# Two column tiles of 256 columns instead of four of 128 in the last two products of a decode step, with two stores for one and four loads of x for five

## The chip, the cores and the metric

The kernel runs on one core of a Trainium2 chip. The metric is the device time of one execution in microseconds (us), given as the median of several runs. A profile is one execution recorded by the hardware; its span is the part between the first and the last recorded work, and the execution's own time is a little longer. The engines are named as in the profile: PE is TensorE (matmul), PEld its weight loads, DVE is VectorE, ACT is ScalarE, POOL is GpSimd and SP is SyncE, which here only issues DMAs. "SPq" and "ACTq" are the instruction queues of SP and ACT as they issue DMAs.

## The reference

One decode step for a batch of 8 rows of 512 numbers, all in bfloat16:

```
xn = layernorm(x)                                   # x: 8 x 512
q  = xn @ wq                                        # 512 x 4096: 32 heads of 128
s  = softmax(q k^T / sqrt(128)) v, last 1024 keys   # 8 key/value heads, each for 4 query heads
s  = s.reshape(8, 4096) @ wo                        # wo: 4096 x 512
f  = (gelu(xn @ w_gate) * (xn @ w_up)) @ w_down     # 512 x 1792, 512 x 1792, 1792 x 512
out = x + s * silu(f)                               # 8 x 512
```

The keys and values that are read are 16 MB each, wq and wo 4 MB each, and the three weights of the second branch 1.75 MB each.

## The kernel before

The order of work on each engine is the order of the program (`tc.manual_schedule()`); nothing reorders it. Tiles in on-chip memory come from pools, and a load into a reused buffer waits until the old content has been read.

**Loads.** ACT issues x first, in five loads of two, two, two, one and one rows (L78, L79). SP issues everything else, in order, on one DMA queue: the first quarter of wo (`wo_first`, L106), wq whole (L109), then the keys and values of the eight batch rows in pieces of 1 MB (`load_cache`, L81 to L90), then w_gate, w_up and w_down (L438, L441), then the rest of wo: two quarters whole and the last in pieces of 5, 2 and 1 of its eight slices (L447 to L451). The large tiles go round in eight buffers (`slot`). The framework has eight semaphores for DMAs and gives them out in turn to the DMAs of the whole program, so that a DMA is not issued before the one eight places ahead of it has landed.

**Layernorm and queries.** DVE takes mean and variance of x (L145, L147), ACT the root (L149), DVE normalizes (L152). PE transposes the result (L167), and spreads x itself over partitions with a matmul (L172) whose result ACT keeps as `x_res` (L179): row b of column block t sits on partition 32t + 4b. The queries are 32 matmuls of 512 columns (L261).

**Attention.** For each batch row: DVE turns the keys over (L249), PE makes the scores (L311), DVE and ACT the softmax (L321 to L333), PE multiplies by the values (L355), and a regrouping on PE and DVE (L376 to L407) leaves the heads' outputs as the stationary operand `oT`.

**The end.** w_gate and w_up are multiplied in four column tiles of 448 columns (L465). A column tile is a stationary operand of 32 columns that uses a quarter of PE's columns, and four of them, with the results on partitions 0, 32, 64 and 96, can run at once. The gelu is a chain of ACT and DVE operations (L475 to L488) that gives `hT`. The product with w_down (L491 to L500) has 14 steps of four column tiles with 128 columns each into `f_ps`. ACT and DVE make silu of it (`g_sb`, L502 to L506). The product with wo (L509 to L519) has 32 steps of the same form into `s_ps`, eight for each quarter of wo. Then DVE multiplies `s_ps` by `g_sb` (L521) and adds `x_res` (L523), and SP stores the result in one DMA that collects 8 rows of 128 columns from each of four partition groups (L525).

Of the kernel before, what the change touches and what calls it, by code (L numbers as in the profile page):

```python
# [10 lines left out]
BF16 = mybir.dt.bfloat16  # L11
FP32 = mybir.dt.float32
# [4 lines left out]
RB = 4  # L17
# [4 lines left out]
def kernel(  # L22
# [13 lines left out]
    nc = tc.nc  # L36

    B, Sq, D = A_x.shape
# [7 lines left out]
    P = nc.NUM_PARTITIONS  # L46
# [4 lines left out]
    ROW = C * Dh  # L51
    FT = F // 4
    NJ = F // P
    DT = D // 4

    ctx.enter_context(tc.manual_schedule())
    consts = ctx.enter_context(tc.tile_pool(name="consts", bufs=1))
    keep = ctx.enter_context(tc.tile_pool(name="keep", bufs=1))
# [16 lines left out]


    x_sb = keep.tile([B, D], BF16, name="x_sb")
    for r, z in ((0, 2), (2, 4), (4, 6), (6, 7), (7, 8)):  # L78
        nc.scalar.dma_start(out=x_sb[r:z], in_=A_x.flatten_outer_dims()[r:z])  # L79

    def load_cache(cache, b, name):  # L81
# [15 lines left out]
    def load_v(b):  # L97
# [21 lines left out]
        out=ident,  # L119
        in_=ident,  # L120
# [13 lines left out]
        out=xpad,  # L134
        in_=xpad,
# [17 lines left out]
        out=xhat,  # L153
# [3 lines left out]
        op0=ALU.subtract,  # L157
        op1=ALU.mult,
    )
    x_res = keep.tile([P, DT], FP32, name="x_res")  # L160
    warm = keep.tile([B, 1], FP32, name="warm")
    nc.scalar.activation(out=warm, in_=rstd, func=ACT.Exp)  # L162
    with tc.tile_pool(name="ps_x", bufs=1, space=PSUM) as ps_x:
        xnT_ps = ps_x.tile([P, NK, B], BF16, name="xnT_ps")
        xv = xhat.rearrange("b (p k) -> b k p", k=NK)
        for k in range(NK):
            nc.tensor.transpose(xnT_ps[:, k, :], xv[:, k, :], ident[0:B, 0:B])  # L167
        for j in range(4):
            nc.vector.tensor_copy(out=xnR[:, :, j, 0 : RB * B : RB], in_=xnT_ps)
        xr_ps = ps_x.tile([P, DT], FP32, name="xr_ps")  # L170
        for t in range(4):
            nc.tensor.matmul(  # L172
                xr_ps[32 * t : 32 * t + 32, :],
                xpad,
                x_sb[:, t * DT : (t + 1) * DT],
                start=True,
                stop=True,
            )
        nc.scalar.copy(out=x_res, in_=xr_ps)  # L179
# [10 lines left out]
        out=hv,  # L190
        in_=hv,
# [7 lines left out]
        out=neg_st,  # L199
        in_=neg_st,  # L200
# [8 lines left out]
        out=neg_mv,  # L209
        in_=neg_mv,  # L210
# [11 lines left out]
    for g in range(NG):  # L222
        nc.vector.tensor_reduce(
            out=sel[:, g, g * qd : (g + 1) * qd],
            in_=ident.rearrange("p (t g h) -> p g h t", t=4, g=NG)[:, g],
# [5 lines left out]
        out=own, in_=ident.rearrange("p (i e) -> p e i", e=8), axis=AX.X, op=ALU.add  # L231
    )
    pick = consts.tile([P, 4 * NU], BF16, name="pick")
    with nc.allow_low_precision(reason="sums of zeros and a single one"):
        nc.vector.tensor_reduce(
            out=pick, in_=ident.rearrange("p (a e) -> p a e", e=8), axis=AX.X, op=ALU.add
# [20 lines left out]
    with tc.tile_pool(name="ps_q", bufs=1, space=PSUM) as ps_q:  # L257
# [10 lines left out]
        for half in range(2):  # L268
            for i in range(4 * half, 4 * half + 4):
                e = nc.vector.tensor_copy if i % 4 == 3 else nc.scalar.copy  # L270
# [7 lines left out]
    for j in range(4):  # L278
        sl = slice(32 * j, 32 * j + 32)
        for m in range(2):  # L280
            for g in range(NG):
                e = nc.scalar.copy if (4 * j + 2 * m + g) % 3 == 2 else nc.vector.tensor_copy
# [160 lines left out]
    for u in range(1, NU):  # L443
        if u % 2 == 1:
            pair = slot("wo_sb").rearrange("p (v j d) -> p v j d", v=2, d=D)
        t = pair[:, (u - 1) % 2]
# [11 lines left out]
    ps_f = ctx.enter_context(tc.tile_pool(name="ps_f", bufs=1, space=PSUM))  # L458
    ffn = ctx.enter_context(tc.tile_pool(name="ffn", bufs=1))
    zu = []  # L460
    for n, ws in (("z_ps", wgu[0]), ("u_ps", wgu[1])):
# [15 lines left out]
        out=z2, in0=z2, scalar1=0.044715, scalar2=1.0, op0=ALU.mult, op1=ALU.add  # L477
# [10 lines left out]
    nc.vector.transpose(  # L488
        out=hT.rearrange("p j b -> p (j b)"), in_=h_bf.rearrange("p (y j) -> p j y", j=NJ)
    )  # L490
    f_ps = ps_f.tile([P, DT], FP32, name="f_ps")  # L491
    for j in range(NJ):
        for t in range(4):
            nc.tensor.matmul(
                f_ps[32 * t : 32 * t + 32, :],
                hT[:, j, :],
                wd[:, j, t * DT : (t + 1) * DT],
                start=(j == 0),
                stop=(j == NJ - 1),
            )  # L500
    g_sb = ffn.tile([P, DT], FP32, name="g_sb")
    nc.scalar.activation(out=g_sb, in_=f_ps, func=ACT.Tanh, scale=0.5)  # L502
    nc.vector.tensor_scalar(
        out=g_sb, in0=g_sb, scalar1=0.5, scalar2=0.5, op0=ALU.mult, op1=ALU.add
# [1 line left out]
    nc.vector.tensor_tensor(out=g_sb, in0=g_sb, in1=f_ps, op=ALU.mult)  # L506


    s_ps = ps_f.tile([P, DT], FP32, name="s_ps")  # L509
    for u in range(NU):  # L510
        for j in range(8):
            for t in range(4):
                nc.tensor.matmul(  # L513
                    s_ps[32 * t : 32 * t + 32, :],
                    oT[:, j, u, :],
                    wo[u][:, j, t * DT : (t + 1) * DT],
                    start=(u == 0 and j == 0),
                    stop=(u == NU - 1 and j == 7),
                )  # L519
    y = ffn.tile([P, DT], FP32, name="y")  # L520
    nc.vector.tensor_tensor(out=y, in0=s_ps, in1=g_sb, op=ALU.mult)  # L521
    out_sb = ffn.tile([P, DT], BF16, name="out_sb")
    nc.vector.tensor_tensor(out=out_sb, in0=y, in1=x_res, op=ALU.add)  # L523
    out_f = out.flatten_outer_dims()
    nc.sync.dma_start(  # L525
        out=out_f.rearrange("b (t d) -> t b d", t=4), in_=out_sb[0 : P : RB, :]
    )


# [28 lines left out]
```

## Time and profile before

| | |
|---|---|
| median of 3 runs | 120.95 us (120.84 to 121.92) |
| the profiled execution's own time | 120.88 us |
| its span | 119.0 us |
| mean granted PE clock | 0.887 of full speed |
| busy share of the span: PE, DVE, ACT, POOL | 61%, 64%, 26%, 3% |
| moved by DMA | 47.60 MB, mean 400 GB/s |

The span is what the views of the profile divide up. The 1.9 us between the span and the own time of the execution lie outside of the record. A row of the timeline has the start in us, the time in us, the engine, the line, the operation, what it writes and reads, how many instructions are merged in the row and, in brackets, how long the engine had been idle and what ended that. A row of the windows view has, for a stretch of time, the busy us of each engine with its instructions in flight, then the granted PE clock as a share of full speed, the mean busy share of the 16 DMA engines, and the GB/s that they moved. Where the page speaks of packets, these are the single pieces that a DMA engine moves; a packet of 4 bytes is the semaphore update at the end of a DMA.

### The profile page before, as it was taken

What the parts mean: (1) busy time and instruction counts of PE and PEld (TensorE: products, weight loads), DVE (VectorE), ACT (ScalarE), POOL (GpSimd) and SP (SyncE); (2) the same over time, 40 slices, a digit from 0 to 9 for tenths busy, and PEclk for the clock granted to TensorE, in tenths of its full rate; (3) what the DMA queues carried; (4) which work ended last, traced back from release to release, by engine and by line L of the source; (5) the groups of instructions that cost most, each with busy time, mean ns of one, the idle gap of its engine ahead of it and who ended that gap; (6) DMA issues with size and microseconds to landing.
All of it is one profiled execution on the core that took longest, in us unless ns stands there. A gap on an engine that the chain in (4) does not pass through costs nothing.

```text
span 119.0 us, 2306 instructions
## 1 busy us (share of the span) xinstructions
PE 72.0 (61%) x992; PEld 37.5 (32%) x992; DVE 75.8 (64%) x101; ACT 31.4 (26%) x75; POOL 3.2 (3%) x10
## 2 busy tenths in 40 slices
PE   0000079941599596979964875698399264844650
PEld 0000033410133253545532434244135253414530
DVE  1000487999999999999957995971994224165100
ACT  1300230096202417170531421151070800120000
POOL 2000052000000000000000000000000000000000
PEclk9999999999679999999999999689859955578595
DMA  2998999999999999999999999999999999999930
GB/s 72 458 507 375 391 421 424 435 427 427 427 430 419 424 435 419 427 430 416 432 424 424 421 430 427 419 435 421 427 424 427 440 434 430 419 431 416 415 138 3
DMA packets 6109, 47.60 MB, mean 400 GB/s; under 512 B 716, under 2 KB 852, under 8 KB 1108
## 3 DMA queue, kind: packets, MB, share of 16 engines
q1 hardware_dynamic: 6084, 47.46, 94.6%
q8 instruction: 7, 0.11, 0.3%
q14 instruction: 2, 0.02, 0.0%
q10 hardware_dynamic: 16, 0.01, 0.0%
HBM read 47.46 MB, written 0.01 MB: 399 GB/s over the span
## 4 chain that ended last, share of the span: by engine, by line
DMA 61%; DVE 15%; PE 15%; ACT 3%; issue 2%; ACTq 1%; DVEq 0%
DMA wo_sb<-in_A_wo_dram 19%; DMA k_sb<-in_A_k_cache_dram 17%; DMA v_sb<-in_A_v_cache_dram 17%; DMA x_sb<-in_A_x_dram 9%; PE q_ps L261 7%; PE S_ps L311 6%; DVE kT L249 6%; DVE qbd L284 2%; DVE mx L321 2%; DVE q_both L274 1%; ACT P_sb L333 1%; ACTq L79 1%; ACT L162 1%; DVE q_both L271 1%; PE O_ps L355 1%
## 5 line engine op out<-in xcount | busy, mean ns | idle before, releaser
L311 PE MATMUL S_ps<-kT,qbd 128*128 128x512 bf16 x128 | 34.8, 420 | 15.4 <-DVE kT L249 12.0
L249 DVE STREAM_TRANSPOSE kT<-k_sb 128x2048 int32<-128x2048 int32 x16 | 36.6, 2289 | 5.0 <-DMA k_sb<-in_A_k_cache_dram 4.9
L311 PEld LDWEIGHTS <-qbd 128*128 128x128 bf16 x128 | 13.0, 103 | 33.3 <-issue 18.0
L331 ACT ACTIVATE nb<-m 32x1 f32<-32x1 f32 x32 | 6.4, 201 | 22.9 <-DVE m L328 22.6
L333 ACT ACTIVATE P_sb<-S_ps,nb 128x1024 bf16<-128x1024 f32 x8 | 11.1, 1391 | 0.3
L355 PE MATMUL O_ps<-v_sb,pT 128*32 128x128 bf16 x512 | 9.5, 231 | 2.6 <-DVE pT L344 2.6
L321 DVE TENSOR_REDUCE mx<-S_ps 128x1 f32<-128x1024 f32 x8 | 9.6, 1195 | 1.7 <-PE S_ps L311 1.6
L355 PEld LDWEIGHTS <-pT 128*32 128x32 bf16 x512 | 8.0, 103 | 5.6 <-issue 3.0
L261 PE MATMUL q_ps<-wq_sb,xnR 128*128 128x512 bf16 x32 | 9.2, 460 | 0.5 <-ACT x_res L179 0.5
L167 PE MATMUL xnT_ps<-ident,xhat 8*128 8x8 bf16 x4 | 0.3, 174 | 15.0 <-DVE xhat L152 15.0
L368 ACT COPY O_sb<-O_ps 128x256 f32<-128x256 f32 x8 | 3.0, 372 | 23.7 <-PE O_ps L355 23.7
L145 DVE BATCH_NORM_STATS2 stats<-x_sb 8x6 f32<-8x512 bf16 x1 | 0.7, 683 | 11.8 <-DMA x_sb<-in_A_x_dram 11.8
L344 DVE STREAM_TRANSPOSE pT<-P_sb 128x512 int32<-128x512 int32 x8 | 5.7, 711 | 3.4 <-ACT P_sb L333 3.3
L376 PE MATMUL o_ps<-O_sb,sel 128*32 128x128 f32 x32 | 5.4, 296 | 1.0 <-ACT O_sb L368 1.0
L300 PE MATMUL S_ps<-neg_mv,neg_st 128*128 128x512 bf16 x16 | 4.8, 381 | 1.9 <-DVE q_both L271 1.9
L261 PEld LDWEIGHTS <-xnR 128*128 128x128 bf16 x32 | 3.6, 114 | 5.8 <-issue 3.0
L271 ACT CAST q_both<-q_ps 128x512 bf16<-128x512 f32 x6 | 3.0, 613 | 7.9 <-PE q_ps L261 7.9
L167 PEld LDWEIGHTS <-xhat 8*128 8x128 bf16 x4 | 0.2, 114 | 15.0 <-DVE xhat L152 15.0
L376 PEld LDWEIGHTS o_ps<-O_sb,sel 128*32 128x32 f32 x32 | 3.0, 115 | 4.7 <-issue 3.2
L513 PE MATMUL s_ps<-wo_sb,oT 128*32 128x128 bf16 x96 | 2.7, 252 | 2.2 <-DMA wo_sb<-in_A_wo_dram 2.2
L252 DVE MEMSET qbd<- 128x4096 uint32 x1 | 3.5, 3472 | 0.8 <-issue 0.8
L513 PEld LDWEIGHTS <-oT 128*32 128x32 bf16 x128 | 3.0, 123 | 2.8 <-issue 2.6
(65 smaller groups left out, 51.1 us busy)
## 6 DMA issues: line engine op xcount, KB each, us to landing
k_sb<-in_A_k_cache_dram SPq DMA_DIRECT2D x16, 1024.0 KB, 19.7
v_sb<-in_A_v_cache_dram SPq DMA_DIRECT2D x16, 1024.0 KB, 19.8
wq_sb<-in_A_wq_dram SPq DMA_DIRECT2D x1, 4096.0 KB, 14.2
wo_sb<-in_A_wo_dram SPq DMA_DIRECT2D x2, 1024.0 KB
wgu_sb<-in_B_w_gate_dram SPq DMA_DIRECT2D x1, 1792.0 KB
wgu_sb<-in_B_w_up_dram SPq DMA_DIRECT2D x1, 1792.0 KB
wd_sb<-in_B_w_down_dram SPq DMA_DIRECT2D x1, 1792.0 KB, 25.1
wo_first<-in_A_wo_dram SPq DMA_DIRECT2D x1, 1024.0 KB, 4.8
```

Of the source, the lines that this page charges most:

```text
L249: nc.vector.transpose(out=t.bitcast(I32), in_=k_sb[b][:, g].bitcast(I32))
L261: nc.tensor.matmul(q_ps[i], xnR[:, k, :, :].rearrange("p j b -> p (j b)"), wq_sb[k][:, i * 512 : (i + 1) * 512], start=(k == 0), stop=(k = ...
L271: e(out=q_bf[:, i * 512 : (i + 1) * 512], in_=q_ps[i])
L300: nc.tensor.matmul(S[b][:, half, :], neg_st.rearrange("p j h -> p (j h)"), neg_mv.rearrange("p a n -> p (a n)"), start=True, stop=False,)
L311: nc.tensor.matmul(S[b][:, half, :], qbd[:, m, b, w, g, :], kv[:, half * 16 : (half + 1) * 16, m, :, w], start=False, stop=(g == NG - 1 an ...
L321: nc.vector.tensor_reduce(out=mx, in_=S[b].rearrange("p a c -> p (a c)"), axis=AX.X, op=ALU.max)
L331: nc.scalar.mul(nb[32 * j : 32 * j + 32, :], m1, -inv)
L333: nc.scalar.activation(out=P_sb[b].rearrange("p c i w -> p c w i"), in_=S[b].rearrange("p a (c w i) -> p (a c) w i", w=2, i=32), func=ACT.Exp,
L344: nc.vector.transpose(out=pT[b].rearrange("p c h w -> p (c h w)").bitcast(I32), in_=P_sb[b].rearrange("p c i w -> p (c i w)").bitcast(I32),)
L355: nc.tensor.matmul(O_ps[b][32 * t : 32 * t + 32, g, :], pT[b][:, c // 2, :, c % 2], vv[:, c, :], start=(c < 4), stop=(c >= C - 4),)
L376: nc.tensor.matmul(o[:, 0:Dh], sel[:, g, :], O_sb[b][:, g, :], start=(g == 0), stop=(g == NG - 1))
L513: nc.tensor.matmul(s_ps[32 * t : 32 * t + 32, :], oT[:, j, u, :], wo[u][:, j, t * DT : (t + 1) * DT], start=(u == 0 and j == 0), stop=(u = ...
```

## The change

The number of column tiles in the products with w_down and wo goes from four to two, and their width from 128 columns to 256. All tiles that follow from it (`x_res`, `xr_ps`, `f_ps`, `g_sb`, `s_ps`, `y`, `out_sb`) go from 128 x 128 to 64 x 256. The store becomes two stores of 8 rows and 256 columns, one issued by SP and one by ACT. The last two loads of x, of one row each, become one of two rows. The products with w_gate and w_up keep their four column tiles.

```diff
-    DT = D // 4
+    NT = 2
+    DT = D // NT
...
-    for r, z in ((0, 2), (2, 4), (4, 6), (6, 7), (7, 8)):
+    for r, z in ((0, 2), (2, 4), (4, 6), (6, 8)):
         nc.scalar.dma_start(out=x_sb[r:z], in_=A_x.flatten_outer_dims()[r:z])
...
-    x_res = keep.tile([P, DT], FP32, name="x_res")
+    x_res = keep.tile([32 * NT, DT], FP32, name="x_res")
...
-        xr_ps = ps_x.tile([P, DT], FP32, name="xr_ps")
-        for t in range(4):
+        xr_ps = ps_x.tile([32 * NT, DT], FP32, name="xr_ps")
+        for t in range(NT):
...
-    f_ps = ps_f.tile([P, DT], FP32, name="f_ps")
+    f_ps = ps_f.tile([32 * NT, DT], FP32, name="f_ps")
     for j in range(NJ):
-        for t in range(4):
+        for t in range(NT):
...
-    g_sb = ffn.tile([P, DT], FP32, name="g_sb")
+    g_sb = ffn.tile([32 * NT, DT], FP32, name="g_sb")
...
-    s_ps = ps_f.tile([P, DT], FP32, name="s_ps")
+    s_ps = ps_f.tile([32 * NT, DT], FP32, name="s_ps")
     for u in range(NU):
         for j in range(8):
-            for t in range(4):
+            for t in range(NT):
...
-    y = ffn.tile([P, DT], FP32, name="y")
+    y = ffn.tile([32 * NT, DT], FP32, name="y")
     nc.vector.tensor_tensor(out=y, in0=s_ps, in1=g_sb, op=ALU.mult)
-    out_sb = ffn.tile([P, DT], BF16, name="out_sb")
+    out_sb = ffn.tile([32 * NT, DT], BF16, name="out_sb")
     nc.vector.tensor_tensor(out=out_sb, in0=y, in1=x_res, op=ALU.add)
     out_f = out.flatten_outer_dims()
-    nc.sync.dma_start(
-        out=out_f.rearrange("b (t d) -> t b d", t=4), in_=out_sb[0 : P : RB, :]
-    )
+    for t, e in ((0, nc.sync), (1, nc.scalar)):
+        e.dma_start(
+            out=out_f[:, t * DT : (t + 1) * DT], in_=out_sb[32 * t : 32 * t + 32 : RB, :]
+        )
```

## The prediction

> **What bounds the kernel now.** I read the page's chain of work first, then the windows view for the DMA share and the granted clock, then the timeline of the last 11 us, and at last the waits and the rows of the tiles that the change touches.
>
> ```profile
> DMA 61%; DVE 15%; PE 15%; ACT 3%; issue 2%; ACTq 1%; DVEq 0%
> ...
> 20.00:30.00 10.00, 5.86 (x26) 2.23 (x23) 9.77 (x15) 5.24 (x10) 0.00 (x0) 1.00 1.01 427
> 60.00:70.00 10.00, 6.78 (x94) 3.57 (x94) 7.70 (x9) 3.09 (x9) 0.00 (x0) 1.00 1.01 424
> 100.00:110.00 10.00, 5.16 (x100) 2.87 (x104) 5.23 (x8) 1.12 (x2) 0.00 (x0) 0.67 1.00 424
> 114.00:115.20 1.20, 0.55 (x26) 0.40 (x26) 0.00 (x0) 0.00 (x0) 0.00 (x0) 1.00 0.36 128
> ```
>
> The last two columns of the windows are the DMA share and GB/s. From 20 to 110 us every stretch has a share of about 1.0 and 424 to 433 GB/s, whatever the other engines do, and the stream ends at 115.1. So the time is the stream plus what is left to do after its last piece. A load of keys lands 17.2 to 20.3 us after its issue (rows of k_sb), so some 17 us of loads are always queued.
>
> ```profile
> 105.00:106.00 1.00, 0.47 (x8) 0.00 (x0) 0.36 (x2) 0.58 (x1) 0.00 (x0) 0.60 0.98 420
> 109.00:110.00 1.00, 1.00 (x60) 1.00 (x52) 0.00 (x0) 0.00 (x0) 0.00 (x0) 0.60 1.03 434
> 112.00:113.00 1.00, 0.08 (x8) 0.08 (x11) 0.00 (x0) 0.00 (x0) 0.00 (x0) 0.69 1.04 415
> ```
>
> The column before the DMA share is the clock. It is 0.50 or 1.00 and changes inside these three stretches: up at 105.8, down at 109.2, up at 112.6, steps of 3.4 us.
>
> ```profile
> 108.80 1.35 PE L494 MATMUL f_ps<-wd_sb,hT 128*32 128x128 bf16 x56 [3.33 <-DVE hT L488]
> 109.92 1.08 PE L513 MATMUL s_ps<-wo_first,oT 128*32 128x128 bf16 x32
> 110.78 1.08 PE L513 MATMUL s_ps<-wo_sb,oT 128*32 128x128 bf16 x32
> 112.92 0.63 PE L513 MATMUL s_ps<-wo_sb,oT 128*32 128x128 bf16 x32 [1.06 <-DMA wo_sb<-in_A_wo_dram]
> 114.47 0.46 PE L513 MATMUL s_ps<-wo_sb,oT 128*32 128x128 bf16 x20 [0.92 <-DMA wo_sb<-in_A_wo_dram]
> 115.11 0.57 PE L513 MATMUL s_ps<-wo_sb,oT 128*32 128x128 bf16 x12 [0.18 <-DMA wo_sb<-in_A_wo_dram]
> 115.73 0.29 DVE L521 TENSOR_TENSOR y<-s_ps,g_sb 128x128 f32<-128x128 f32 x1 [4.61 <-PE s_ps L513]
> 116.06 0.29 DVE L523 TENSOR_TENSOR out_sb<-y,x_res 128x128 bf16<-128x128 f32 x1
> 116.38 0.70 SPq L525 DMA_DIRECT2D out_dram<-out_sb  x1
> ```
>
> PE waits three times for wo, 2.16 us in all: that is its whole slack. The last piece of wo releases the last four matmuls at 115.44, DVE adds two operations, and the store is issued from 116.38 to 117.08. The trace's packet records have its 32 packets of 256 bytes from 117.68 to 117.84 and the last update at 117.86. SP sees it at 118.21, and 0.8 us of closing work ends the span.
>
> **The change, part by part.** The sum is made against the profiled execution, 120.88 us, which is 0.07 under the median of 120.95.
>
> The PE products. Eight steps of four tiles take from 109.92 to 110.78, 0.107 us a step at clock 0.50; at 112.92, (0.63 - 0.22 of the last matmul) over nearly eight steps, 0.055 us at 1.00. A 512-column matmul (L311) takes 1.91 us for eight at full clock, (1.91 - 0.38)/7 = 0.219, four times as much: the step goes by columns. Two tiles of 256 columns then cost 0.213 us a step at half clock and 0.107 at full. There are 14 + 32 = 46 steps. With the clock as in this execution: from 108.80 to 109.20 at full clock 3.8 steps, to 112.62 at half clock 16, so w_down ends at 111.4 and the first half of wo is partly done; the other 26.2 steps at full clock take 2.8 us, to 115.4. The last piece comes at 115.44. So the slack is used up nearly to the last step, and the end moves only by the longer last step: +0.05. Cover gone, it would cost the 46 steps' doubling, 2.5 us at full clock and 4.9 at half. g_sb would be ready near 113.0 (f_ps at 111.8, then ACT and two DVE operations of 0.3 to 0.43), 2.7 us before L521 needs it; today it is ready at 111.1.
>
> The two last DVE operations have 256 columns instead of 128. The same operation takes 0.29 us on 128 columns and 0.62 on 448 (L479, L483), 1.03 ns a column, so each becomes 0.42. Both are on the path: +0.27. L502, L503 and L506 grow likewise behind the wait for wo, at nothing; cover gone, 0.3.
>
> The store. The issue has 0.70 us for 4 x 8 pieces. Nearest rows for a plain one: ACT's loads of two rows, 0.24 to 0.27 us, the first of them 0.54; SP's loads of 128 rows, 0.33. I take 0.33 on SP, nearest in engine and place, and 0.24 to 0.54 on ACT, beside it. From end of issue to first packet 0.60 here, and 0.39 for the first load of x; I keep 0.60. The packets: 32 on four engines (four updates) in 0.17 us become eight of 512 bytes in each store, one to an engine if it follows the old pattern; a packet of 1024 bytes takes 0.046 us, so 0.05 with its update, -0.12. In sum -0.37 - 0.12, and 0.04 back for a second store among the closing waits (SP's waits stand 0.06 apart): -0.45. Bounds: -0.79 (issue 0.24, latency 0.39, packets 0.05) and +0.1 (ACT at 0.54 or more, a wait more, the rest unchanged). ACT has nothing queued behind its store, and its last work before, g_sb, is long done.
>
> The Trainium skill speaks against this gain: "DMA: Bandwidth & Descriptors", section "Anatomy of one DMA", puts the fixed cost of a small DMA at about 2 us, nearly all of it the receipt of the last byte. Here the store takes 1.83 us from issue to SP's release, near that, but 0.70 of it is the issue and only 0.35 comes after the last packet.
>
> x in four loads.
>
> ```profile
> L79 ACTq DMA_DIRECT2D x_sb<-in_A_x_dram x5: 243/273/542, 0.8 to 2.3; - x5
> ...
> SPq L84 <- DMA x_sb<-in_A_x_dram: 5.1, 3, 1.9
> ...
> 16.03 4.43 PE L261 MATMUL q_ps<-wq_sb,xnR 128*128 128x512 bf16 x10 [0.52 <-ACT x_res L179]
> ...
> DMA to landing us min/median/max: 14.2/14.2/14.2
> ```
>
> The issues end at 2.6, and x is complete only at 12.7: in the packet records each load of x has its rows, and 1.2 us later its update, between the large packets of wo and wq; the fourth load has its row at 8.95 and its update at 10.20, the fifth at 11.41 and 12.66. Without the fifth, x is there 2.5 us sooner. But the queries also need wq, which lands 14.2 us after its issue at 1.26, at 15.46, and today they start at 16.03. So at most 0.57 us is won there, and the stream, with 17 us of loads queued, hides it: 0. Cover gone, it is worth -0.2 (the matmuls run at half clock until 20.5 anyway) to -0.57. SP's early loads waited 5.1 us for landings of x, through the shared semaphores; one load less lets some go 1 to 2 us sooner, into a full queue: 0. The steady spacing of eight DMAs in flight is the same. L172 and L179 have half the instructions or twice the columns, long before they are needed: 0.
>
> Sum: 120.88 + 0.05 + 0.27 - 0.45 = 120.75, on the median's scale 120.8. The likeliest case reaches from 120.4 to 121.2 with the store's bounds.
>
> **Rivals.**
> *The clock's steps fall elsewhere.* The steps of 3.4 us need not stand the same to the program each time. A step with PE 78% busy (109.2 to 112.6) was followed by full clock, one with 72% (95.6 to 99.0) was not. If the step that begins after PE's start at 108.8 begins at 109.5 to 111.4, the clock is half from 108.8 to 112.9 to 114.8, and the 46 steps end 0.2 to 1.1 us behind the last piece of wo: 121.0 to 121.9. Chance 0.25. For the forecast speaks that this profile's own phase gives no delay.
>
> *PE stays at half clock: slower.* Full clock comes only after a busy step, and no row shows whether two column tiles of four count as fully busy; all busy stretches of narrow tiles here had four. If they count half, the clock stays 0.50 from 109.2, and 42.2 steps of 0.213 us end at 118.2, 2.7 us late: 123.5. It decides from the point at which two tiles fall under the share that was enough, between 72% and 78%. Chance 0.14, because the timeline would have PE busy without a gap. "TensorE: Matmul & The Clock Gate" of the Trainium skill, Part 1, says that the gate goes by how busy PE has been in windows of about 3.4 us; the 3.4 us agrees, and what counts as busy no run here shows.
>
> *The store gains nothing.* ACT's first issue after 113 us without one costs 0.54 as its first load of x did, and the rest is fixed: 120.88 + 0.32 = 121.2. Against it speaks the 0.70 of the issue, which the plain loads lack. Chance 0.15; that is also the time by the skill's fixed cost above.
>
> *The gain is larger.* The store's low bound, 120.4, or the earlier queries reach the end after all, 120.2. Speaking for it: each was worked out from rows; against: the stream's share of 1.0. Chance 0.08.
>
> **How the numbers follow.** 0.38 is left for the forecast, 120.8. 1% is about what a measurement of this kernel can tell from no change, 1.2 us: under 119.7 faster, over 122.2 slower. Slower are the half-clock rival, 0.14, and 0.06 of late steps together with a store that gains nothing. Faster needs more than any term gives, 0.04. The rest, 0.76, is within 1%. The range, 120.2 to 122.3, takes in the bounds of the store and the late steps, and leaves out the half-clock rival and 0.06 more.
>
> **What would show it.** In the profile after: steps of L494 and L513 at 0.107 and 0.213 us; the waits of PE for wo gone but for the last piece; clock 1.00 from about 112.6; L521 and L523 at 0.42; issues of 0.33 and under 0.54 and SP's release about 1.4 us after the issue; x landed near 10.5, the queries begun near 15.5, and the stream's end still at 115. A last wo piece that lies ready while PE works behind it, or a clock of 0.50 past 113, would make the prediction wrong; so would a stream that ends elsewhere.

## The result

The changed kernel takes 121.50 us (median of 22 runs, 121.32 to 122.01), the kernel before 120.94 us (22 runs, 120.84 to 122.52): a ratio of 1.0044, 95% interval 1.003 to 1.0059. By the ratio it is 0.53 us slower. The profiled execution took 121.32 us with a span of 119.46, against 120.88 and 119.02: 0.44 more.

The timeline of the end of the changed kernel (columns as before):

```profile
108.39 3.17 PE L495 MATMUL f_ps<-wd_sb,hT 128*32 128x256 bf16 x28 [2.94 <-DVE hT L489]
111.35 1.08 PE L514 MATMUL s_ps<-wo_first,oT 128*32 128x256 bf16 x16
112.26 1.91 PE L514 MATMUL s_ps<-wo_sb,oT 128*32 128x256 bf16 x32
114.44 1.26 PE L514 MATMUL s_ps<-wo_sb,oT 128*32 128x256 bf16 x16 [0.27 <-DMA wo_sb<-in_A_wo_dram]
115.73 0.42 DVE L522 TENSOR_TENSOR y<-s_ps,g_sb 64x256 f32<-64x256 f32 x1 [2.92 <-PE s_ps L514]
116.19 0.42 DVE L524 TENSOR_TENSOR out_sb<-y,x_res 64x256 bf16<-64x256 f32 x1
116.63 0.80 SPq L527 DMA_DIRECT2D out_dram<-out_sb  x1
116.64 0.74 ACTq L527 DMA_DIRECT2D out_dram<-out_sb  x1
```

L521 of before is L522 here. It starts at 115.73 in both profiled executions, so nothing ahead of it moved the end there. PE's three waits for wo, 2.16 us, have shrunk to one of 0.27. At the end of the program SP passes six waits for semaphores, one after the other; they are called the closing waits here. From 115.73 on three things differ:

| | before | after | difference |
|---|---|---|---|
| the two DVE operations, until the store's issue | 0.65 | 0.90 | +0.25 |
| from the issue to the last packet's record (an update of 4 bytes) | 1.48 | 1.58 | +0.10 |
| from there until SP has passed its last closing wait | 0.35 | 0.44 | +0.09 |

The 0.81 us behind that are the same. The three rows make the 0.44 us of the profiled executions; 0.09 of the 0.53 is not in them, and the last experiments come back to it. The stores' issues, 0.80 and 0.74 us, are no shorter than the one of 0.70 that they replace. The second row has three parts, here for SP's store: its issue (0.70 before, 0.80 after), the flight from the end of the issue to its first packet (0.60 and 0.69), and its packets with their updates (0.18 and 0.09).

The windows of the changed kernel, where the column before the DMA share is the clock:

```profile
110.00:111.00 1.00, 1.00 (x14) 0.69 (x12) 0.00 (x0) 0.00 (x0) 0.00 (x0) 0.50 1.00 422
111.00:112.00 1.00, 1.00 (x18) 0.82 (x16) 0.00 (x0) 0.38 (x1) 0.00 (x0) 0.79 0.99 416
112.00:113.00 1.00, 1.00 (x22) 0.90 (x20) 0.70 (x2) 0.00 (x0) 0.00 (x0) 1.00 0.96 391
```

PE is busy without a gap, and the clock goes up inside the second stretch, at 111.4. At the start of the kernel the rows of x and of the queries read:

```profile
L80 ACTq DMA_DIRECT2D x_sb<-in_A_x_dram x4: 249/273/553, 0.8 to 2.0; - x4
L146 DVE BATCH_NORM_STATS2 stats<-x_sb x1: 682/682/682, 10.6 to 10.6; 8x6 f32<-8x512 bf16 x1
...
15.49 8.91 PE L262 MATMUL q_ps<-wq_sb,xnR 128*128 128x512 bf16 x32 [2.37 <-DMA wq_sb<-in_A_wq_dram]
```

The statistics of x begin at 10.6 instead of 13.1, and the queries now wait for wq, to 15.49.

### The profile page after: what moved, and what is told of

It reads as the page before. It is cut to its first block, busy times and chain, and to the rows that moved or that the text cites. A ratio compares the mean times of both kernels' runs of the same rounds, so it can differ in the third digit from the quotient of the medians.

```text
span 119.5 us, 2119 instructions
## 1 busy us (share of the span) xinstructions
PE 71.1 (59%) x898; PEld 38.2 (32%) x898; DVE 76.3 (64%) x101; ACT 31.6 (26%) x75; POOL 3.2 (3%) x10
## 4 chain that ended last, share of the span: by engine, by line
DMA 94%; PE 1%; DVE 1%; ACTq 1%; issue 0%; SPq 0%
DMA v_sb<-in_A_v_cache_dram 69%; DMA wo_sb<-in_A_wo_dram 20%; DMA x_sb<-in_A_x_dram 5%; PE s_ps L514 1%; ACTq L80 1%; DVE y L522 0%; DVE out_sb L524 0%; SPq L452 0%
## 5 line engine op out<-in xcount | busy, mean ns | idle before, releaser
L312 PE MATMUL S_ps<-kT,qbd 128*128 128x512 bf16 x128 | 31.4, 389 | 18.9 <-DVE kT L250 15.5
L312 PEld LDWEIGHTS <-qbd 128*128 128x128 bf16 x128 | 12.5, 98 | 34.9 <-issue 18.4
L495 PE MATMUL f_ps<-wd_sb,hT 128*32 128x256 bf16 x28 | 3.2, 419 | 2.9 <-DVE hT L489 2.9
```

The lines of the kernel that those rows point to most:

```text
L312: nc.tensor.matmul(S[b][:, half, :], qbd[:, m, b, w, g, :], kv[:, half * 16 : (half + 1) * 16, m, :, w], start=False, stop=(g == NG - 1 an ...
```

## The experiments

The question was why two plain stores are not cheaper to issue than one of 32 pieces, and whether anything but the last 3 us matters. Theory A at first: a store's issue costs 0.7 us whatever its shape. Its rivals: two stores do save (B), or a first issue on a cold queue is what is dear (C).

**x alone (x_four).** The kernel before with the diff's line of x, nothing else.

> The kernel before with only the x part of the change: four loads of x. Theory (the tail alone slowed the change): x is complete at 10.2 us in place of 12.7, the queries start at 15.5 in place of 16.0, the stream of loads still ends at 115.1 and the time is that of before, within 0.1 us. Rival (the x part moves the stream or the shared semaphores): 0.2 us or more in either direction, and the stream's end moves with it.

Measured: 121.05 us (12 runs), ratio 0.9998 (0.9985 to 1.0012). The interval allows no effect over about 0.2 us, and the median shows none, as all theories of the tail need.

**One store (one_store).** The changed kernel with

```diff
-    for t, e in ((0, nc.sync), (1, nc.scalar)):
-        e.dma_start(
-            out=out_f[:, t * DT : (t + 1) * DT], in_=out_sb[32 * t : 32 * t + 32 : RB, :]
-        )
+    nc.sync.dma_start(
+        out=out_f.rearrange("b (t d) -> t b d", t=NT), in_=out_sb[0 : 32 * NT : RB, :]
+    )
```

> The changed kernel with one store on SP that collects 8 rows from both partition groups, in place of two plain stores. Theory A (the issue of a store costs 0.7 us or more whatever its shape, and two at once take 0.1 longer than one): the issue is 0.70, the time 0.1 us under the changed kernel's. Theory B (two stores side by side do save, and the tail lost its time elsewhere): 0.1 to 0.4 us over the changed kernel's.

Measured: 121.27 us (12 runs), ratio 1.0023 (1.0007 to 1.0039), half of the changed kernel's loss. The two column tiles alone cost 0.28 us by the ratio, close to the 0.25 of the two DVE operations. What is left of the loss points to the second store, but the two intervals overlap, and the spans of the two profiles differ by 0.12 us only (119.34 and 119.46). Theory B falls. The timeline of its store:

```profile
116.63 0.68 SPq L526 DMA_DIRECT2D out_dram<-out_sb  x1
```

**A store early and again (store_twice).** In the changed kernel, ahead of the tile `g_sb`:

```diff
+    out_f = out.flatten_outer_dims()
+    for t, e in ((0, nc.sync), (1, nc.scalar)):
+        e.dma_start(
+            out=out_f[:, t * DT : (t + 1) * DT], in_=h_bf[32 * t : 32 * t + 32 : RB, 0:DT]
+        )
```

> The changed kernel with a store like each of the two issued also once before, from the hidden layer's tile near 107.5 us, on SP and on ACT; the final stores overwrite it. Theory A (a store's issue costs 0.7 to 0.8 us by itself): early and late stores both take that, and the time is the changed kernel's, 0 to 0.1 over. Theory C (the issue is long because the queue has issued nothing like it before, or nothing for 20 us): the late ones take 0.25 to 0.4, and the time is 0.4 us under the changed kernel's.

Measured: 122.17 us (6 runs), ratio 1.0081 (1.0057 to 1.0105). The rows of the output in its trace, early issues (L504) and late ones (L532):

```profile
L504 SPq DMA_DIRECT2D out_dram<-h_bf x1: 797/797/797, 107.6 to 107.6; - x1
L504 ACTq DMA_DIRECT2D out_dram<-h_bf x1: 733/733/733, 107.6 to 107.6; - x1
L532 SPq DMA_DIRECT2D out_dram<-out_sb x1: 693/693/693, 117.1 to 117.1; - x1
L532 ACTq DMA_DIRECT2D out_dram<-out_sb x1: 652/652/652, 117.1 to 117.1; - x1
```

A repeated issue is 0.1 us shorter, so theory C explains 0.1 of 0.7 and no more. The loss of 0.6 us over the changed kernel (by the medians; 0.45 by the ratios) was not expected. Two causes are in the trace. The late stores land 1.75 us after their issue, where the changed kernel's take 1.58, and SP passes the wait for one of them as the second of its six, with four more waits behind. And PE is late:

```profile
108.60:113.40 4.80, 4.77 (x46) 3.54 (x48) 0.70 (x2) 0.38 (x1) 0.00 (x0) 0.50 1.00 418
113.40:116.20 2.80, 2.73 (x50) 2.24 (x46) 0.02 (x1) 0.00 (x0) 0.00 (x0) 1.00 0.33 121
```

Here the clock stays at 0.50 until 113.4; its steps of 3.4 us begin elsewhere than in the changed kernel's profile. PE works from 108.6 to 116.1 without a wait, and L527, the first DVE operation of the tail, starts at 116.18, 0.45 us later than in the changed kernel. That is what the prediction's first rival describes; the mean granted clock of this execution is 0.872.

**Two half stores of four tiles (halves).** The kernel before with

```diff
-    nc.sync.dma_start(
-        out=out_f.rearrange("b (t d) -> t b d", t=4), in_=out_sb[0 : P : RB, :]
-    )
+    out_v = out_f.rearrange("b (t d) -> t b d", t=4)
+    for h, e in ((0, nc.sync), (1, nc.scalar)):
+        e.dma_start(
+            out=out_v[2 * h : 2 * h + 2], in_=out_sb[64 * h : 64 * h + 64 : RB, :]
+        )
```

> The kernel before, four column tiles and five loads of x, with its store in two halves, two column tiles each, on SP and ACT at once. Theory A: issues of 0.70 to 0.80 each, 32 packets on two queues, the time 0 to 0.1 us over before. Theory B (half the pieces, a cheaper issue): issues of 0.35 to 0.5, the time 0.2 to 0.35 us under before.

Measured: 121.31 us (12 runs), ratio 1.0018 (1.0004 to 1.0033); issues of 0.684 and 0.639:

```profile
L527 SPq DMA_DIRECT2D out_dram<-out_sb x1: 684/684/684, 116.5 to 116.5; - x1
L527 ACTq DMA_DIRECT2D out_dram<-out_sb x1: 639/639/639, 116.5 to 116.5; - x1
```

So 32, 16 and 8 pieces all cost 0.64 to 0.80 us to issue: the number of pieces is not the price. Theory A expected 0 to 0.1 and the ratio makes 0.22: the second store costs something behind the issue too. SP is through the wait for one of the two, the third of its six, at 118.52, and three waits follow; before, SP is through its last at 118.24.

**What an issue costs (probes).** Behind the activation of L503 of the changed kernel, with `scr_a` and `scr_b` new tiles and `x_f` the rows of x:

```diff
...
+    nc.scalar.dma_start(out=scr_a, in_=x_f[:, 0:DT])
+    nc.scalar.dma_start(out=scr_b[0:32:RB, :], in_=x_f[:, DT : 2 * DT])
+    nc.scalar.dma_start(out=out_f[:, 0:DT], in_=h_bf[0:B, 0:DT])
+    nc.scalar.dma_start(out=out_f[:, DT : 2 * DT], in_=h_bf[0:32:RB, 0:DT])
```

> The changed kernel with four DMAs more on ACT, after its last activation, only to read their issue times: eight rows of x to eight neighbouring partitions, eight rows of x to every fourth partition, a store from eight neighbouring partitions, a store from every fourth; the two stores write rows of the output that the final stores overwrite. If a store's issue is dear because it is a store: the loads take 0.25 to 0.35, the stores 0.65 to 0.8. If the step over partitions is dear: the second and fourth take 0.65 or more, the others 0.25 to 0.35. If eight rows over eight engines are dear: all four take 0.65 or more. If only a cold queue is: the first takes 0.5 to 0.8 and the rest about 0.3.

One run was made, of 121.73 us; only its issues are read. The timeline of the four, in this order, and of the final store on ACT:

```profile
111.85 0.28 ACTq L508 DMA_DIRECT2D scr_a<-in_A_x_dram  x1
112.17 0.73 ACTq L509 DMA_DIRECT2D scr_b<-in_A_x_dram  x1
...
113.00 0.41 ACTq L510 DMA_DIRECT2D out_dram<-h_bf  x1
113.45 1.25 ACTq L511 DMA_DIRECT2D out_dram<-h_bf  x1
...
116.71 0.63 ACTq L535 DMA_DIRECT2D out_dram<-out_sb  x1
```

All four move 8 rows of 256 columns. The load to every fourth partition takes 0.45 us more to issue than the load to neighbouring ones. The store from neighbouring partitions takes 0.41, and every store from every fourth partition so far 0.63 or more. Theory A falls: in these rows it is the step over partitions that is dear, for the load as for the stores. (The 1.25 us of the fourth is longer than any other such issue, 0.58 to 0.80; it was issued right behind another store, and what held it was not tried.)

**The same two stores without the step (packed_two).** The changed kernel with batch row b on partition 32t + b in place of 32t + 4b:

```diff
+    xnF = keep.tile([P, NK, 32], BF16, name="xnF")
+    nc.vector.memset(xnF, 0.0)
...
-        channel_multiplier=RB,
+        channel_multiplier=1,
...
+        nc.vector.tensor_copy(out=xnF[:, :, 0:B], in_=xnT_ps)
...
-            out=oT[:, :, :, 4 * RB * q : 4 * RB * (q + 1) : RB],
+            out=oT[:, :, :, 4 * q : 4 * (q + 1)],
...
-                    xnR[:, k, t, :],
+                    xnF[:, k, :],
...
-            ..., in_=out_sb[32 * t : 32 * t + 32 : RB, :]
+            ..., in_=out_sb[32 * t : 32 * t + B, :]
```

> The changed kernel with the batch rows of the last products on neighbouring partitions, 32t + b in place of 32t + 4b, so that each of the two plain stores reads eight neighbouring partitions; a packed copy of the normalized x serves w_gate and w_up, one small DVE copy more near 15 us. If the step over partitions makes the issue dear: issues of 0.30 to 0.45, the time 0.3 to 0.45 us under the changed kernel's, ratio to before 1.000 to 1.002. If the step has no part in it: issues of 0.7 to 0.8 and a ratio of 1.004 as before.

Measured: 120.90 us (12 runs, 120.82 to 121.32), ratio to before 1.0001 (0.9991 to 1.0011). The loss is gone. The timeline:

```profile
115.79 0.42 DVE L525 TENSOR_TENSOR y<-s_ps,g_sb 64x256 f32<-64x256 f32 x1 [2.68 <-PE s_ps L517]
116.24 0.42 DVE L527 TENSOR_TENSOR out_sb<-y,x_res 64x256 bf16<-64x256 f32 x1
116.68 0.37 SPq L530 DMA_DIRECT2D out_dram<-out_sb  x1
116.69 0.30 ACTq L530 DMA_DIRECT2D out_dram<-out_sb  x1
```

The issues take 0.37 and 0.30, and the last update is recorded at 117.64, 0.96 us after the issue, where the changed kernel has 1.58 and before 1.48. The flight of SP's store is shorter too: its first packet comes 0.46 us after the end of its issue, where the changed kernel has 0.69 and before 0.60.

**Four plain stores (packed_each).** The kernel before, packed in the same way, with

```diff
+    for t, e in ((0, nc.sync), (2, nc.scalar), (1, nc.sync), (3, nc.scalar)):
+        e.dma_start(
+            out=out_f[:, t * DT : (t + 1) * DT], in_=out_sb[32 * t : 32 * t + B, :]
+        )
```

> The kernel before, four column tiles and five loads of x, packed in the same way, with one plain store of 8 rows and 128 columns for each column tile, two on SP and two on ACT one after the other. If the step is what costs: 0.3 to 0.45 for each issue, 0.7 to 0.9 for the two of a queue, so the time is that of before, 0 to 0.25 us over (another wait among the closing ones). If a store costs 0.7 whatever it reads: 1.4 for the two, 0.7 us over.

Measured: 121.46 us (10 runs), ratio 1.0041 (1.0015 to 1.0068).

```profile
L529 SPq DMA_DIRECT2D out_dram<-out_sb x2: 298/328/357, 116.4 to 116.8; - x2
L529 ACTq DMA_DIRECT2D out_dram<-out_sb x2: 298/304/309, 116.4 to 116.7; - x2
```

The price of an issue without the step is confirmed four times, 0.30 to 0.36. The time was missed by 0.25 us. The last update is recorded at 117.70, ahead of before's 117.86, but SP passes the first of its six closing waits, which is for one of these stores, only at 118.20, 0.49 us later, and the rest follow 0.06 apart. (This profiled execution took 122.71 us, far more than the other nine, but its span of 119.3 is no longer than theirs of 119.4 and 119.5.)

**The order of the closing waits (early_store, x_four_early, packed_each_x2).** early_store is the kernel before with its store, from `h_bf`, issued once more near 106 us; x_four_early has four loads of x as well; packed_each_x2 is packed_each with x in two loads of four rows.

> The kernel before with its store, in the same form, issued once more near 107 us from the hidden layer's tile; the final store overwrites it. If a first store of its form pays 0.1 us that a second doesn't: the late issue takes 0.60 and the time is 0.05 to 0.1 us under before. If it is the price of the store itself: 0.70 and no gain, or a loss of up to 0.3 us by the 32 packets in the stream and the wait for their landing.

> The kernel before with four loads of x and with its store issued once early. The early store alone shortened the late issue from 0.70 to 0.58, but put the late store on a semaphore that SP waits for ahead of three others, 0.06 each. One load of x less moves the late store to the semaphore waited for last. If that reading is right: issue 0.58, no more than one wait behind the landing, 0.05 to 0.12 us under before. If the place among the waits means nothing: 0.15 us over before, as with the early store alone.

> Four column tiles, packed, with four plain stores, and x in two loads of four rows: three DMAs less ahead of the stores, which moves them to the semaphores that SP waits for last. Four stores with five loads of x gave 1.0041, with the last packet at 117.70, yet SP passed the first of its six closing waits only at 118.20. If the order of the waits cost the difference: five of the waits are over before the stores land, the ratio is 0.998 to 1.000. If four landings in themselves are slow: 1.003 to 1.004 as before.

Measured: 121.15 us (11 runs), ratio 1.0015 (1.0006 to 1.0024); 121.05 us (11 runs), 1.0008 (0.9999 to 1.0016); 121.24 us (10 runs), 1.003 (1.0015 to 1.0044). The rows of the stores of early_store:

```profile
L502 SPq DMA_DIRECT2D out_dram<-h_bf x1: 697/697/697, 106.3 to 106.3; - x1
L529 SPq DMA_DIRECT2D out_dram<-out_sb x1: 581/581/581, 116.6 to 116.6; - x1
```

The late issue is 0.12 us shorter, as expected, and 0.59 in x_four_early, but neither kernel is faster than before. The place of the waits moved as expected (in early_store three waits stand behind the store's, in x_four_early none), but the difference of the two ratios, 0.0007, is smaller than the half-width of either interval. In packed_each_x2 the four stores are on the last four waits, and SP passes them at 117.64, 117.84, 118.04 and 118.24, 0.2 us apart instead of 0.06. Its profiled execution, at 121.03, is one of its fastest, and the scatter up to 121.87 isn't explained by it. So the order of the waits is not the cause that I took it for: with four stores it does not remove the loss, and whether it has a part in it (121.24 against 121.46, with overlapping intervals), or with one store, is not settled.

**PE kept busy (pe_filled, packed_filled).** Six matmuls of 512 columns between the products with w_up and w_down, in the changed and in the packed kernel:

```diff
+    idle_ps = ps_f.tile([P, 512], FP32, name="idle_ps")
+    for i in range(6):
+        nc.tensor.matmul(
+            idle_ps,
+            xnR[:, i % NK].rearrange("p j b -> p (j b)"),
+            wgu[1][:, i % NK, 0:512],
+            start=(i == 0),
+            stop=(i == 5),
+        )
```

> The changed kernel with six more matmuls of 512 columns on PE between w_up's product and w_down's, into a result of their own that nothing reads. They fill PE's idle stretch from 105.5 to 108.2 us, so that the clock is up when w_down's product starts, or soon after. If late PE steps at half clock cost the changed kernel time in some runs: the runs over 121.6 go, and the median falls by 0.1 to 0.2 us to about 121.35. If PE never delays the end, or two narrow tiles keep the clock up just as well: the median and the spread of the changed kernel's runs (121.3 to 122.0) stay. If the clock does not rise for two tiles, nothing changes either, but the clock column stays at 0.50.

> The packed two-tile kernel with the six idle matmuls on PE ahead of w_down's product, which nothing reads. The packed kernel had eight runs at 120.82 to 120.92 and four at 121.13 to 121.32. If the later group is PE working behind the last piece of wo at half clock: no such group here, all runs within 0.15 us of their median. If it has another cause (the stream's end): a group 0.3 us later stays, one run in three.

Measured: 121.60 us (5 runs, 121.46 to 121.71), ratio 1.0048 (1.0034 to 1.0062); 120.89 us (12 runs, 120.72 to 121.72), ratio 0.9995 (0.9976 to 1.0014). In pe_filled the clock is up from 109.9 and PE waits for wo again, 0.54 and 0.50 us, but the median does not fall; in its profile the last piece of wo releases PE at 115.59, 0.18 us later than in the changed kernel's, and why is open. In packed_filled two of twelve runs lie 0.26 and 0.83 over the median, where none was expected.

The mean granted clock of each run hints at how often PE was late. Of the changed kernel's 22 runs, eight have the 0.872 of store_twice's profile, and these take 121.64 to 122.01 us. The other fourteen take 121.32 to 121.55, but for one of 121.76, and their median is 121.42. So the late steps of PE add 0.08 us to the median, if this clock stands for them in these eight runs as it does in the one that has a profile. Three of the four runs of packed_two above 121.1 have 0.871; pe_filled and packed_filled, with the clock up early, have no run under 0.891. The late runs at other clocks have at least one other cause, which stays open.

## Why the prediction was wrong

The range held the time, but the sign was wrong: 0.1 us faster was forecast, 0.53 slower measured. Point by point:

- *The bound, the stream:* right. It ends at 115.03 in the changed kernel's packet records, 115.06 before.
- *x in four loads, 0:* right, by x_four. x is complete at 10.1 and the queries begin at 15.49, as worked out. (That a load's update comes 1.2 us behind its rows holds for the last three of the five loads of before; for the first two it is 0.04.)
- *The PE steps:* right in size. The 28 matmuls of w_down take 3.17 us, 0.21 a step, at half clock, the 16 of wo from 111.35 to 112.26 take 0.11 a step. The slack is used up to 0.27 us, and L522 starts where L521 did. That the end did not move is in part luck of the phase: PE began 0.41 us sooner than in the sum, and the clock went up at 111.4 instead of 112.6. The eight runs at a clock of 0.872 lie 0.2 to 0.6 us over the median of the others; if the clock reads them rightly, the first rival came true in these.
- *PE stays at half clock:* fell. Two tiles of four are enough: the clock went up at 111.4, after PE had been busy for 3.04 us of the 3.41 from 108.01. The rule of busy windows in the Trainium skill's "TensorE: Matmul & The Clock Gate", Part 1, agrees. But the share between 72% and 78% that the prediction took for the limit is not borne out: from 101.18 to 104.60 PE was busy for 2.75 of 3.42 us, 80%, and half clock followed. What a busy step needs stays open.
- *The two DVE operations, +0.27:* right, 0.42 each, +0.25.
- *The store, -0.45:* **the step that failed.** It was +0.19 (0.10 to the last update, 0.09 in the closing waits), and even its upper bound of +0.1 was too low. Its largest term, the issue, was put at -0.37 and measured +0.10; the packets, put at -0.12, made -0.09, and the flight, taken as unchanged, +0.09. The issue was priced by loads of neighbouring partitions, 0.33 on SP, "nearest in engine and place", and the 0.70 of before was put down to its 32 pieces. But the changed stores still read every fourth partition. The probes price that step at 0.45 us; without it the issues are 0.37 and 0.30 and the last update comes 0.52 us sooner than before. So the price of 0.33 was right for another access pattern than that of these stores. That 0.52 is close to the predicted 0.49 is luck beyond the issue: the packets gave 0.04 there and not 0.12, and the flight, which the prediction left unchanged, gave 0.14.
- *The second store among the closing waits, +0.04:* too small. With one store SP is through 0.35 us after the last update, with two 0.44 (after) and 0.50 (packed_two): the wait for the second is passed 0.19 and 0.18 us after that for the first, where other waits stand 0.06 apart.

With the store at +0.19 in place of -0.45 the prediction's own sum is 120.88 + 0.05 + 0.27 + 0.19 = 121.39; the runs without late PE steps have a median of 121.42, and all of them 121.50. By its number the first rival, 121.0 to 121.9, takes this in, but most of the loss is not its mechanism. The rival "the store gains nothing", 121.2, was the nearest in what it says of the store, but its reason, a dear first issue on ACT, is worth 0.1 us at most by store_twice.

The Trainium skill's "DMA: Bandwidth & Descriptors", section "Anatomy of one DMA", with a nearly constant 2 us for a small DMA, gave a sum nearer to the result than mine did, but not for its reason. Its fit is one of DMAs issued by GpSimd. From issue to SP's release it is 2.02 us here, 1.83 before and 1.46 in packed_two; of the 0.56 between the first and the last, 0.43 is the issue, and the time behind the last update is 0.06 longer in packed_two, not shorter.

No version was measured to be faster than before: packed_two is equal to it. One single store from neighbouring partitions, which would have the short issue without a second closing wait, was not tried.

## What to carry to other kernels

Price an operation by a row with the same access pattern, not the same engine: "plain" was a word for the output's side of these stores, and the side in on-chip memory kept its step. A store at the end of a program is worth looking at in three parts, the issue, the flight and the closing waits; neighbouring partitions shortened the issue of SP's store by 0.43 us and its flight by 0.23, and the second store made the closing waits about 0.1 us longer. Work that fills another engine's slack to the last step costs nothing in one profile, but it ties the end to where that engine's clock steps fall.

## What the runs showed of the hardware

A DMA between every fourth partition and the rows of x or of the result took 0.58 to 0.80 us to issue (once 1.25), one of eight rows on neighbouring partitions 0.28 to 0.41, for a load and for stores, on SP and ACT; with the step, 8, 16 and 32 pieces cost alike. An issue of the same form repeated later in the program was 0.1 us shorter (0.80 to 0.69, 0.70 to 0.58). The engines that a store uses show in the packet records as updates of 4 bytes: 4 for the one store of before, 8 for each of the two of the changed kernel, 2 for that of one_store, which agrees with the rule in the Trainium skill's "DMA: Bandwidth & Descriptors", section "Why a DMA increments its semaphore by 16 and not by 1", that the count divides the slowest dimension of both sides.
